# A two-layer squared-ReLU block on one core: the start of block 0, the loads of w1 and the shifted copies of x rearranged

## The chip, the core and the metric

The kernel runs on one core of a Trainium2 chip. The metric is the device time of one execution in microseconds (us), lower is better. The profile's span, from the first to the last instruction, is about 2 us shorter than that time (295.2 against 297.05 us for the profiled run).

Engines are named as in the profile: PE is TensorE's matmuls, PEld its weight loads, DVE is VectorE, ACT is ScalarE, POOL is GpSimd, SP is SyncE. SPq, ACTq and POOLq are their queues, which issue DMA transfers.

## What is computed

```python
# x [1, 2048, 576], w1 [576, 4608], b1 [4608], w2 [4608, 576], b2 [576], all bf16
h = jnp.einsum("bsd,df->bsf", x, w1) + b1
r = jnp.where(h > 0, h, 0)
h = r * r
out = jnp.einsum("bsf,fd->bsd", h, w2) + b2
```

The depth of the first product, 576, is four and a half times 128; that odd half shapes the whole kernel.

## The kernel before

The 2048 rows of x are cut into four blocks of 512 columns of the transposed x. The 4608 columns of w1 are cut into 36 f-tiles of 128. Phase A makes hT = relu(...)^2 for each block and f-tile; phase B multiplies hT with w2.

The depth of 576 is nine chunks of 64. TensorE is used as two halves of 64 rows: the lower 64 partitions work on one f-tile, the upper 64 on another, at the same time, each into a PSUM bank of its own. So w1 lies in SBUF as `w1h`: 64 partitions per half, nine chunks, and a step handles a pair of f-tiles. In the kernel before, pair j is f-tiles j and j + 18, as `w1h`'s lower half holds the first half of w1's columns and its upper half the second.

```python
P = 128; H = 64; NFT = 36; NJ = 18; NC = 4; NH = 9; DM = 512; SB = 512; NSB = 4; RT = 4; HALF = 256
def load_w1(eng, j0, j1):                   # two transfers of 64 partitions each
    for h in range(2):
        eng.dma_start(out=w1h[h * H:(h + 1) * H, :, j0 * P:j1 * P],
                      in_=w1_rows[:, :, h * FH + j0 * P:h * FH + j1 * P])
# ... cut ...
ORDER = ((0, 2, 4, 6, 8, 1, 3, 5, 7), (1, 3, 5, 7, 8, 2, 4, 6, 0))
def a_step(b, j):                           # one pair: 18 matmuls of 64 rows, two evictions
    bk = [bank("ph") for _ in range(2)]
    for i in range(NH):
        for h in range(2):
            c = ORDER[h][i]
            rows = slice(h * H, (h + 1) * H)
            nc.tensor.matmul(bk[h][:], lhsT=w1h[rows, c, j * P:(j + 1) * P],
                             rhs=xT[b][rows, place(h, c), :],
                             start=(i == 0), stop=(i == NH - 1))
    for h in range(2):
        evac_h(b, h * NJ + j, bk[h])        # ACT: relu + b1; DVE: square into hT
```

Each half needs all nine chunks of x on its own 64 partitions. Loaded naturally, even chunks lie on the lower half and odd ones on the upper, so some chunks have to be copied ("shifted") to the other half. For blocks 1 to 3 x comes by DMA transposes that fetch most of it twice, and two chunks are left to copy on VectorE at the start of each block:

```python
for b in range(1, NSB):
    nc.vector.tensor_copy(out=xT[b][0:H, 8, :], in_=xT[b][H:P, 7, :])   # line 228
    nc.vector.tensor_copy(out=xT[b][H:P, 8, :], in_=xT[b][0:H, 0, :])   # line 229
    for j in range(NJ):
        a_step(b, j)
    # ... cut: loads of w2 ...
```

Block 0 starts before transposed x and w1h are there. It loads x as it is (four tiles of 128 rows) and a "quad" of f-tiles as full 128-row chunks; it transposes x on TensorE, half a block (256 columns) at a time, and computes the quad with full-height matmuls. The last 64 rows of depth (the tail) are done with half-height ones. Chunk number 4 of `transpose_chunk` covers the last 128 columns of x and holds this tail in its upper half.

```python
quad = (0, 1, NJ, NJ + 1)                   # f-tiles 0, 1, 18, 19
load_x(nc.sync, 0);    load_x(nc.scalar, 1)
load_quad(nc.sync, 0); load_quad(nc.scalar, 1)   # each: 128 rows x two runs of 256 columns (512 B)
load_quad(nc.sync, 2); load_quad(nc.scalar, 3)
load_x(nc.sync, 2);    load_x(nc.sync, 3)
# ... cut: tail of the quad, identity, b1 and the tail of b2 by GpSimd, six warm-up matmuls ...
steps = [(half, c) for half in range(2) for c in range(NC + 1)]
transpose_chunk(0, 0, engs[0])              # two TensorE transposes, then a copy out of PSUM
for i, (half, c) in enumerate(steps):       # on VectorE and ScalarE in turn
    if i + 1 < len(steps):
        transpose_chunk(*steps[i + 1], engs[(i + 1) % 2])
    if c < NC:
        full_mm(half, c)                    # line 178: four matmuls of 256 columns
    elif half == 0:
        ...                                 # transposes b1 once
nc.vector.tensor_copy(out=xT[0][0:H, 8, :], in_=xT[0][H:P, 7, :])       # line 193, the tail
nc.vector.tensor_copy(out=xT[0][0:H, 4:7, :], in_=xT[0][H:P, 0:3, :])   # shifted copies
nc.vector.tensor_copy(out=xT[0][H:P, 4:7, :], in_=xT[0][0:H, 1:4, :])
nc.vector.tensor_copy(out=xT[0][H:P, 8, :], in_=xT[0][0:H, 0, :])
# ... cut: four tail matmuls (line 200) and the quad's evictions ...
for j0, j1 in ((2, 4), (4, 6), (6, 9), (9, 13), (13, 18), (0, 2)):
    load_w1(nc.sync, j0, j1)
# ... cut: DMA transposes of x for blocks 1 to 3, loads of b2 and w2, all on SyncE ...
for j in range(2, NJ):
    a_step(0, j)
```

Phase B is not changed, but for the column that holds b2's last 64 values and the place where block 3's hT lies (over w1h, by the pair's number).

Of the kernel before, what the change touches and what calls it, by code (L numbers as in the profile page):

```python
# [9 lines left out]
ACT = mybir.ActivationFunctionType  # L10
ALU = mybir.AluOpType
BF16 = mybir.dt.bfloat16
FP32 = mybir.dt.float32
# [4 lines left out]
def kernel(  # L18
# [9 lines left out]
    nc = tc.nc  # L28
    P = 128
    H = 64  # L30
    x2 = x.flatten_outer_dims()
    out2 = out.flatten_outer_dims()
    S, D = x2.shape
    F = w1.shape[1]
    FH = F // 2
    NFT = F // P
    NJ = NFT // 2
    NC = D // P
    NH = D // H
    DM = NC * P  # L40
    SB = 512
    NSB = S // SB
    RT = SB // P
    HALF = SB // 2
    XW = NH * SB
    assert D == DM + H and NH == 9 and NSB == 4 and NFT % 2 == 0

    ctx.enter_context(tc.manual_schedule())
    const = ctx.enter_context(tc.tile_pool(name="const", bufs=1))
# [6 lines left out]
    def bank(name):  # L56
        return psum.tile([P, SB], FP32, name=name, tag="bank")

    w1h = big.tile([P, NH, FH], BF16, name="w1h")
    hT = [big.tile([P, NFT, SB], BF16, name=f"hT{b}") for b in range(NSB - 1)]

    w2_sb = big.tile([P, NFT * D], BF16, name="w2_sb")
    at = [0]

    def early(n):
        at[0] += n
        assert at[0] <= NFT * D
        return w2_sb[:, at[0] - n:at[0]]  # L70


    xT = [early(XW).rearrange("p (w s) -> p w s", s=SB) for b in range(NSB - 1)]
# [2 lines left out]
    xs = early(RT * D).rearrange("p (j c) -> p j c", c=D)  # L76
    qn = early(NC * 4 * P).rearrange("p (c f) -> p c f", c=NC)
    qr = early(2 * P)
    quad = (0, 1, NJ, NJ + 1)

    x_view = x2.rearrange("(rt p) d -> p rt d", p=P)
    w1_halves = w1.rearrange("d (h f) -> d h f", h=2)
    w1_rows = w1.rearrange("(c p) f -> p c f", p=H)

    def w2(ft, a, b):
        return w2_sb[:, ft * D + a:ft * D + b]

    def load_x(eng, j):
        eng.dma_start(out=xs[:, j, :], in_=x_view[:, j, :])

    def load_quad(eng, c):
        eng.dma_start(out=qn[:, c, :].rearrange("p (h f) -> p h f", h=2),
                      in_=w1_halves[c * P:(c + 1) * P, :, 0:2 * P])

    def load_w1(eng, j0, j1):
        for h in range(2):
            eng.dma_start(out=w1h[h * H:(h + 1) * H, :, j0 * P:j1 * P],
                          in_=w1_rows[:, :, h * FH + j0 * P:h * FH + j1 * P])

    load_x(nc.sync, 0)  # L100
    load_x(nc.scalar, 1)
    load_quad(nc.sync, 0)
    load_quad(nc.scalar, 1)
    load_quad(nc.sync, 2)
    load_quad(nc.scalar, 3)
    load_x(nc.sync, 2)
    load_x(nc.sync, 3)
    for h in range(2):
        nc.sync.dma_start(out=qr[h * H:(h + 1) * H, :], in_=w1_halves[DM:D, h, 0:2 * P])

    ident = const.tile([P, P], BF16, name="ident")
    make_identity(nc, ident[:])
    b1_rows = const.tile([P, P], BF16, name="b1_rows")
    nc.gpsimd.memset(b1_rows[:], 0.0)
    nc.gpsimd.dma_start(out=b1_rows[0:NFT, :], in_=b1.rearrange("(ft p) -> ft p", p=P))
    for h in range(2):
        nc.gpsimd.dma_start(out=b1_rows[NFT:NFT + 1, h * H:(h + 1) * H],
                            in_=b2[DM:D].rearrange("(o d) -> o d", o=1))

    ones = nc.const_aps.tensor(1.0, [P, SB], BF16)  # L120
    wps = bank("wps")
# [4 lines left out]
    def copy_psum(eng, dst, src):  # L126
        if eng is nc.scalar:
            nc.scalar.copy(out=dst, in_=src)  # L128
        else:
            nc.vector.tensor_copy(out=dst, in_=src)  # L130

    def transpose_chunk(half, c, eng):
        d0 = c * P if c < NC else D - P
        cols = slice(half * HALF, (half + 1) * HALF)
        tp = psum.tile([P, HALF], BF16, name="tp", tag="bank")
        for i in range(2):
            nc.tensor.transpose(tp[:, i * P:(i + 1) * P], xs[:, 2 * half + i, d0:d0 + P], ident[:])  # L137
        copy_psum(eng, xT[0][:, c if c < NC else 7, cols], tp[:])

    def hT_of(b, ft):  # L140
        if b < NSB - 1:
            return hT[b][:, ft, :].rearrange("p (j s) -> p j s", j=RT)
        h, j = divmod(ft, NJ)
        return w1h[:, h * RT:(h + 1) * RT, j * P:(j + 1) * P]

    b1T = const.tile([P, NFT + 1], FP32, name="b1T")

    def evac_h(b, ft, bk):
        r = rpool.tile([P, SB], BF16, name="r", tag="r")
        nc.scalar.activation(out=r[:], in_=bk[:], func=ACT.Relu, bias=b1T[:, ft:ft + 1], scale=1.0)  # L150
        r3 = r[:].rearrange("p (j s) -> p j s", j=RT)
        nc.vector.tensor_tensor(out=hT_of(b, ft), in0=r3, in1=r3, op=ALU.mult)  # L152

    def place(hi, c):
        if hi:
            return c // 2 if c % 2 else (3 + c // 2 if c else 8)
        return 8 if c == 8 else (4 if c % 2 else 0) + c // 2

    ORDER = ((0, 2, 4, 6, 8, 1, 3, 5, 7), (1, 3, 5, 7, 8, 2, 4, 6, 0))

    def a_step(b, j):
        bk = [bank("ph") for _ in range(2)]
        for i in range(NH):
            for h in range(2):
                c = ORDER[h][i]
                rows = slice(h * H, (h + 1) * H)
                nc.tensor.matmul(bk[h][:], lhsT=w1h[rows, c, j * P:(j + 1) * P], rhs=xT[b][rows, place(h, c), :],  # L167
                                 start=(i == 0), stop=(i == NH - 1))
        for h in range(2):
            evac_h(b, h * NJ + j, bk[h])  # L170


    bk0 = [bank("ph") for _ in quad]

    def full_mm(half, c):
        cols = slice(half * HALF, (half + 1) * HALF)
# [2 lines left out]
                             start=(half == 0 and c == 0), stop=False, skip_group_check=True)  # L179

    engs = (nc.vector, nc.scalar)
    steps = [(half, c) for half in range(2) for c in range(NC + 1)]
    transpose_chunk(0, 0, engs[0])
    for i, (half, c) in enumerate(steps):
        if i + 1 < len(steps):
            transpose_chunk(*steps[i + 1], engs[(i + 1) % 2])
        if c < NC:
            full_mm(half, c)
        elif half == 0:
            b1T_ps = psum.tile([P, P], BF16, name="b1T_ps", tag="bank")  # L190
            nc.tensor.transpose(b1T_ps[:], b1_rows[:], ident[:])
            nc.vector.tensor_copy(out=b1T[:], in_=b1T_ps[:, 0:NFT + 1])
    nc.vector.tensor_copy(out=xT[0][0:H, 8, :], in_=xT[0][H:P, 7, :])
    nc.vector.tensor_copy(out=xT[0][0:H, 4:7, :], in_=xT[0][H:P, 0:3, :])
    nc.vector.tensor_copy(out=xT[0][H:P, 4:7, :], in_=xT[0][0:H, 1:4, :])
    nc.vector.tensor_copy(out=xT[0][H:P, 8, :], in_=xT[0][0:H, 0, :])
    for i in range(2):
        for h in range(2):
            rows = slice(h * H, (h + 1) * H)
            nc.tensor.matmul(bk0[2 * h + i][:], lhsT=qr[rows, i * P:(i + 1) * P], rhs=xT[0][rows, place(h, 8), :],  # L200
                             start=False, stop=True, skip_group_check=True)
        for h in range(2):
            evac_h(0, quad[2 * h + i], bk0[2 * h + i])


    for j0, j1 in ((2, 4), (4, 6), (6, 9), (9, 13), (13, 18), (0, 2)):
        load_w1(nc.sync, j0, j1)
    for b in range(1, NSB):
        rows = slice(b * SB, (b + 1) * SB)
        for i in range(2):  # L210
            nc.sync.dma_start_transpose(out=xT[b][:, i * NC:(i + 1) * NC, :], in_=x2[rows, i * H:i * H + DM])
    w2_view = w2_dram.rearrange("(ft p) d -> p ft d", p=P)
    W2CH = 6

    def load_w2(c):
        nc.sync.dma_start(out=w2_sb[:, c * W2CH * D:(c + 1) * W2CH * D].rearrange("p (ft d) -> p ft d", d=D),
                          in_=w2_view[:, c * W2CH:(c + 1) * W2CH, :])
# [2 lines left out]
    nc.sync.dma_start(out=b2_bc[:], in_=b2[0:DM].partition_broadcast(P))  # L220
    load_w2(4)
    load_w2(5)

    for j in range(2, NJ):
        a_step(0, j)
    load_w2(0)
    for b in range(1, NSB):
        nc.vector.tensor_copy(out=xT[b][0:H, 8, :], in_=xT[b][H:P, 7, :])  # L228
        nc.vector.tensor_copy(out=xT[b][H:P, 8, :], in_=xT[b][0:H, 0, :])
        for j in range(NJ):  # L230
            a_step(b, j)
        if b == 1:
            load_w2(1)
        if b == 2:
            load_w2(2)
            load_w2(3)


    oc = xpool.tile([P, NH, SB], BF16, name="oc", tag="xT3")
    o_tr = []  # L240
    for pr in range(NSB // 2):
        pc = bank("pc")
        for ft in range(NFT):
            for h in range(2):
                nc.tensor.matmul(pc[h * H:(h + 1) * H, :], lhsT=w2(ft, DM, D), rhs=hT_of(2 * pr + h, ft),  # L245
                                 start=(ft == 0), stop=(ft == NFT - 1))
        nc.scalar.activation(out=oc[:, pr, :], in_=pc[:], func=ACT.Identity, bias=b1T[:, NFT:NFT + 1], scale=1.0)  # L247
        o_tr.append(oc[:, 2 + pr, :].rearrange("p (j r) -> p j r", j=RT))
        nc.sync.dma_start_transpose(out=o_tr[pr], in_=oc[:, pr, :])

# [48 lines left out]
```

## Time and profile before

| what | value |
|---|---|
| time, median of 3 | 297.96 us (297.69 to 299.83) |
| span of the profiled run | 295.2 us |
| PE busy | 285.6 us, 97% |
| first full-height matmul of block 0 | 5.47 us after the span's start |
| first paired step | 11.46 us |
| end of phase A, first matmul of phase B | 152.08 us |
| DMA moved | 18.01 MB, mean 61 GB/s |

In the page and the views, a line of instructions gives start and duration in us, engine, source line, operation, output<-inputs, shape and count; what stands in brackets at the end is the idle time of that engine just before and what ended it. "Busy" for PE counts pipelined matmuls with modelled ends, so two matmuls in a row overlap; the cadence is read from starts, not from durations. A few matmul records are missing from a trace, so counts may be a little short.

### The profile page before, as it was taken

Reading aid. Unit: us, or ns where it says so; the run is one execution under the profiler, and the core shown is the slowest. Engines: PE = TensorE matmul, PEld = TensorE weight load, DVE = VectorE, ACT = ScalarE, POOL = GpSimd, SP = SyncE. Lnnn points to the kernel's source line nnn. Section 1 sums busy time; section 2 is a strip of 40 time slices with the busy share of each in tenths; the row PEclk is TensorE's granted clock in tenths of the full one; section 3 lists DMA queues with packets and bytes.
Section 4 is the critical chain, followed back from the end, with each engine's and each line's share of the span. In section 5 each row is a group of like instructions: output and inputs, shape, how many; then the busy total and the mean of one; then the engine's idle time right before and its main releaser. Section 6 shows DMA issues by size and latency. Waiting matters only on the chain.

```text
span 295.2 us, 4817 instructions
## 1 busy us (share of the span) xinstructions
PE 285.6 (97%) x2079; PEld 141.7 (48%) x2079; DVE 78.8 (27%) x193; ACT 95.5 (32%) x152; POOL 2.5 (1%) x10
## 2 busy tenths in 40 slices
PE   6999998999899998999999999999999999999996
PEld 3654444555455554555555444444444444444454
DVE  0644444444444445344440011000111111111111
ACT  2666665666656665566650000000000000000000
POOL 3000000000000000000000000000000000000000
PEclk9999999999999999999999999999999999999999
DMA  6999998910120003400000000000000000000000
GB/s 183 205 201 201 171 197 171 307 59 2 34 88 0 3 0 99 143 2 0 2 0 13 7 20 20 20 23 20 20 20 22 20 20 20 22 20 20 20 22 21
DMA packets 29909, 18.01 MB, mean 61 GB/s; under 512 B 14516, under 2 KB 29888, under 8 KB 29888
## 3 DMA queue, kind: packets, MB, share of 16 engines
q1 hardware_dynamic: 29104, 17.29, 26.3%
q10 hardware_dynamic: 688, 0.41, 0.5%
q8 instruction: 16, 0.26, 0.4%
q14 instruction: 5, 0.04, 0.0%
q0 software_dynamic: 96, 0.01, 0.0%
HBM read 11.94 MB, written 2.36 MB: 48 GB/s over the span
## 4 chain that ended last, share of the span: by engine, by line
PE 59%; DVE 0%; issue 0%
PE po L259 42%; PE ph L167 12%; PE pc L245 5%; DVE o_sb L261 0%
## 5 line engine op out<-in xcount | busy, mean ns | idle before, releaser
L150 ACT ACTIVATE r<-ph,b1T 128x512 bf16<-128x512 f32 x144 | 90.9, 684 | 51.8 <-PE ph L167 51.1
L167 PE MATMUL ph<-w_sb,w1h 64*128 64x512 bf16 x936 | 101.9, 376 | 2.4 <-DVE w_sb L228 2.3
L167 PEld LDWEIGHTS <-w1h 64*128 64x128 bf16 x1260 | 69.9, 94 | 70.7 <-issue 4.7
L259 PE MATMUL po<-w_sb,hT 128*128 128x512 bf16 x432 | 93.4, 379 | 0.0
L259 PEld LDWEIGHTS <-hT 128*128 128x128 bf16 x432 | 42.2, 98 | 51.2 <-issue 0.4
L152 DVE TENSOR_TENSOR hT<-r 128x512 bf16<-128x512 bf16 x108 | 45.9, 425 | 58.0 <-ACT r L150 57.7
L261 DVE TENSOR_TENSOR o_sb<-po,b_bc 128x512 bf16<-128x512 f32 (+2 forms) x17 | 11.2, 660 | 116.7 <-PE po L259 116.7
L167 PE MATMUL ph<-xT,w1h 64*128 64x512 bf16 x324 | 35.3, 376 | 1.3 <-DVE xT L228 1.3
L259 PE MATMUL po<-w_sb,w1h 128*128 128x512 bf16 (+2 forms) x180 | 31.3, 336 | 0.0
L259 PEld LDWEIGHTS <-w1h 128*128 128x128 bf16 x180 | 16.2, 98 | 15.3
L152 DVE TENSOR_TENSOR w1h<-r 128x512 bf16<-128x512 bf16 x36 | 15.3, 425 | 20.4 <-ACT r L150 20.4
L245 PE MATMUL pc<-hT,w_sb 128*64 128x512 bf16 x108 | 15.7, 379 | 0.0
L245 PEld LDWEIGHTS <-w_sb 128*64 128x64 bf16 x144 | 8.1, 110 | 7.6 <-issue 0.4
L245 PE MATMUL pc<-w1h,w_sb 128*64 128x512 bf16 x36 | 7.9, 379 | 0.0
L178 PE MATMUL ph<-w_sb 128*128 128x256 bf16 x32 | 4.6, 272 | 2.0 <-DMA w_sb<-in_w_dram 1.7
L247 ACT ACTIVATE oc<-pc,b1T 128x512 bf16<-128x512 f32 x2 | 1.4, 687 | 13.8 <-PE pc L245 13.8
L255 DVE COPY o_sb<-oc 128x64 bf16<-128x64 bf16 x16 | 2.7, 172 | 9.4 <-DMA oc<-oc 9.4
L178 PEld LDWEIGHTS <-w_sb 128*128 128x128 bf16 x32 | 2.9, 97 | 2.5 <-DMA w_sb<-in_w_dram 1.8
L130 DVE COPY w_sb<-tp 128x256 bf16<-128x256 bf16 x5 | 1.5, 291 | 8.0 <-PE tp L137 8.0
L128 ACT COPY w_sb<-tp 128x256 bf16<-128x256 bf16 x5 | 1.9, 373 | 5.0 <-PE tp L137 4.9
L124 PE MATMUL wps<-const-bfloat16-1.0 128*128 128x512 bf16 x6 | 2.7, 623 | 0.8 <-PEq L283 0.8
L137 PE MATMUL tp<-ident,w_sb 128*128 128x128 bf16 x20 | 2.6, 228 | 0.0
(25 smaller groups left out, 11.3 us busy)
## 6 DMA issues: line engine op xcount, KB each, us to landing
w_sb<-in_w_dram SPq DMA_DIRECT2D x6, 864.0 KB, 7.6
out_dram<-o_sb SPq DMA_DIRECT2D x15, 144.0 KB, 1.8
w1h<-in_w_dram SPq DMA_DIRECT2D x6, 288.0 KB, 6.3
w1h<-in_w_dram SPq DMA_DIRECT2D x2, 720.0 KB, 16.9
w1h<-in_w_dram SPq DMA_DIRECT2D x2, 576.0 KB, 13.4
w1h<-in_w_dram SPq DMA_DIRECT2D x2, 432.0 KB, 9.0
w_sb<-in_x_dram SPq DMA_DIRECT2D x3, 144.0 KB, 3.4
w_sb<-in_w_dram ACTq DMA_DIRECT2D x2, 128.0 KB, 3.7
```

The costliest lines, as they stand in the source:

```text
L124: nc.tensor.matmul(wps[:], lhsT=ones[:, 0:P], rhs=ones[:], start=(i == 0), stop=(i == NWARM - 1))
L128: nc.scalar.copy(out=dst, in_=src)
L130: nc.vector.tensor_copy(out=dst, in_=src)
L137: nc.tensor.transpose(tp[:, i * P:(i + 1) * P], xs[:, 2 * half + i, d0:d0 + P], ident[:])
L150: nc.scalar.activation(out=r[:], in_=bk[:], func=ACT.Relu, bias=b1T[:, ft:ft + 1], scale=1.0)
L152: nc.vector.tensor_tensor(out=hT_of(b, ft), in0=r3, in1=r3, op=ALU.mult)
L167: nc.tensor.matmul(bk[h][:], lhsT=w1h[rows, c, j * P:(j + 1) * P], rhs=xT[b][rows, place(h, c), :], start=(i == 0), stop=(i == NH - 1))
L178: nc.tensor.matmul(bk0[q][:, cols], lhsT=qn[:, c, q * P:(q + 1) * P], rhs=xT[0][:, c, cols], start=(half == 0 and c == 0), stop=False, ski ...
L245: nc.tensor.matmul(pc[h * H:(h + 1) * H, :], lhsT=w2(ft, DM, D), rhs=hT_of(2 * pr + h, ft), start=(ft == 0), stop=(ft == NFT - 1))
L255: nc.vector.tensor_copy(out=o_sb[:, DM:D], in_=o_tr[pr][:, jj, h * H:(h + 1) * H])
L259: nc.tensor.matmul(po[:, 0:e - a], lhsT=hT_of(b, ft)[:, jj, :], rhs=w2(ft, a, e), start=(ft == 0), stop=(ft == NFT - 1))
L261: nc.vector.tensor_tensor(out=o_sb[:, a:e], in0=po[:, 0:e - a], in1=b2_bc[:, a:e], op=ALU.add)
```

## The change

Five things are moved at once; the arithmetic is the same, apart from the order in which partial sums are added.

1. Block 0's quad is f-tiles 0 to 3, neighbours in memory, so a row of a quad load is one run of 1 KB. The pairs follow: (0, 2), (1, 3), and then f with f + 4 in groups of four.
2. w1 comes in groups of four pairs with runs of 1 KB (two pairs last). The lower halves are issued on SyncE, the upper halves on GpSimd, the first group in two parts (five and four chunks). These loads are issued early in the program, before the warm-up matmuls; x's fourth tile moves from SyncE's queue to ScalarE's.
3. In block 0's start, the tail chunk is transposed second instead of last, and its shifted copy is taken straight out of PSUM. The remaining shifted copies of block 0 are no longer ahead of the tail matmuls.
4. Pairs 2 to 5 of block 0 run their first five steps one pair after the other, and then their last four, in eight banks, so that the chunks that need a shifted copy come later.
5. The two copies that complete x for block b + 1 move from the start of that block to the middle of block b (for block 1: after pair 14 of block 0). b2's last 64 values get a column of their own.

```diff
-    quad = (0, 1, NJ, NJ + 1)
+    pairs = [(0, 2), (1, 3)] + [(f, f + G) for f in range(G, NFT) if (f // G) % 2]     # G = 4
     def load_quad(eng, c):
-        eng.dma_start(out=qn[:, c, :].rearrange("p (h f) -> p h f", h=2),
-                      in_=w1_halves[c * P:(c + 1) * P, :, 0:2 * P])
+        eng.dma_start(out=qn[:, c, :], in_=w1[c * P:(c + 1) * P, 0:G * P])
-    load_x(nc.sync, 3)
+    load_x(nc.scalar, 3)
+    def load_w1(eng, h, j0, n, cs):
+        f0 = pairs[j0][h] * P
+        eng.dma_start(out=w1h[h * H:(h + 1) * H, cs, j0 * P:(j0 + n) * P], in_=w1_rows[:, cs, f0:f0 + n * P])
+    w1_first = ((slice(0, 9, 2), slice(1, 8, 2)), (slice(1, 8, 2), slice(0, 9, 2)))
+    for part in range(2):
+        for h, eng in enumerate((nc.sync, nc.gpsimd)):
+            load_w1(eng, h, 2, G, w1_first[h][part])
+    for m in range(1, 4):
+        for h, eng in enumerate((nc.sync, nc.gpsimd)):
+            load_w1(eng, h, 2 + G * m, G, slice(0, NH))
 ... cut ...
         copy_psum(eng, xT[0][:, c if c < NC else 7, cols], tp[:])
+        if c == NC:
+            nc.vector.tensor_copy(out=xT[0][0:H, 8, cols], in_=tp[H:P, :])
 ... cut ...
-    steps = [(half, c) for half in range(2) for c in range(NC + 1)]
-    transpose_chunk(0, 0, engs[0])
-    for i, (half, c) in enumerate(steps):
-        if i + 1 < len(steps):
-            transpose_chunk(*steps[i + 1], engs[(i + 1) % 2])
-        if c < NC:
-            full_mm(half, c)
+    n = 0
+    for half in range(2):
+        ahead = [0, NC, 1, 2, 3]
+        lead = 3 if half == 0 else 2
+        for i in range(lead):
+            transpose_chunk(half, ahead[i], engs[n % 2])
+            n += 1
+        for c in range(NC):
+            full_mm(half, c)
+            if lead + c < NC + 1:
+                transpose_chunk(half, ahead[lead + c], engs[n % 2])
+                n += 1
 ... cut: b1's transpose after half 0; the four tail matmuls ...
-    nc.vector.tensor_copy(out=xT[0][0:H, 8, :], in_=xT[0][H:P, 7, :])      # was ahead of the tail matmuls
+    # the other shifted copies of block 0 stand after the tail matmuls
-    for j0, j1 in ((2, 4), (4, 6), (6, 9), (9, 13), (13, 18), (0, 2)):
-        load_w1(nc.sync, j0, j1)
+    for h, eng in enumerate((nc.sync, nc.gpsimd)):
+        load_w1(eng, h, 0, 2, slice(0, NH))
 ... cut ...
-    for j in range(2, NJ):
-        a_step(0, j)
+    bks = {}
+    for j in range(2, 2 + G):
+        bks[j] = [bank("ph") for _ in range(2)]
+        a_part(0, j, bks[j], range(5))          # a_part: the given steps of a_step's loop
+    for j in range(2, 2 + G):
+        a_part(0, j, bks[j], range(5, NH))
+        for h in range(2):
+            evac_h(0, pairs[j][h], bks[j][h])
+    for j in range(2 + G, NJ):
+        a_step(0, j)
+        if j == NJ - 4:
+            finish_xT(1)                        # finish_xT(b): the two copies of lines 228 and 229
     for b in range(1, NSB):
-        nc.vector.tensor_copy(out=xT[b][0:H, 8, :], in_=xT[b][H:P, 7, :])
-        nc.vector.tensor_copy(out=xT[b][H:P, 8, :], in_=xT[b][0:H, 0, :])
         for j in range(NJ):
             a_step(b, j)
+            if j == NJ // 2 and b + 1 < NSB:
+                finish_xT(b + 1)
```

The aims: longer runs and two issuing queues for w1, work for TensorE while the shifted copies of block 0 are made, and no copies at the seams between blocks.

## The prediction

> **What bounds the kernel now.** I read the page's busy shares first, then the list of waits, then TensorE's own timeline, then a table of stages for the DMA rate.
>
> ```profile
> span 295.2 us, 4817 instructions
> PE 285.6 (97%) x2079; PEld 141.7 (48%) x2079; DVE 78.8 (27%) x193; ACT 95.5 (32%) x152; POOL 2.5 (1%) x10
> ```
>
> TensorE is busy 285.6 of 295.2 us. The change removes no matmul, so it can only take from the 9.6 us in which TensorE stands idle, or spend more of them. The list of waits says where they are:
>
> ```profile
> PE ph L167 <- DVE w_sb L228: 2.3, 2, 1.2
> ...
> PE ph L178 <- DMA w_sb<-in_w_dram: 1.7, 1, 1.7
> PE ph L167 <- DVE xT L228: 1.3, 1, 1.3
> ...
> PEld L167 <- DMA w1h<-in_w_dram: 0.5, 1, 0.5
> ```
>
> (Columns: us in total, times, longest us.) Three stalls at the starts of blocks 1, 2 and 3, behind the shifted x copy of line 228, sum to 3.6 us. One stall of 1.7 us is for the first w1 quad. The only wait for w1h itself is 0.5 us, and that is on the weight-load side, so w1's supply does not bound block 0. TensorE's timeline puts the stalls in order (start, length, what, idle before):
>
> ```profile
> 3.29 0.52 PE L137 MATMUL tp<-ident,w_sb 128*128 128x128 bf16 x4
> 5.47 0.61 PE L178 MATMUL ph<-w_sb 128*128 128x256 bf16 x4 [1.66 <-DMA w_sb<-in_w_dram]
> ...
> 7.80 0.28 PE L137 MATMUL tp<-ident,w_sb 128*128 128x128 bf16 x2
> 8.37 0.60 PE L178 MATMUL ph<-w_sb 128*128 128x256 bf16 x4 [0.29 <-ACT w_sb L128]
> ...
> 11.03 0.61 PE L200 MATMUL ph<-w_sb 64*128 64x512 bf16 x4 [0.35 <-DVE w_sb L193]
> 11.46 32.54 PE L167 MATMUL ph<-w_sb,w1h 64*128 64x512 bf16 x296
> 45.09 35.14 PE L167 MATMUL ph<-w_sb,w1h 64*128 64x512 bf16 x324 [1.09 <-DVE w_sb L228]
> 81.48 34.28 PE L167 MATMUL ph<-w_sb,w1h 64*128 64x512 bf16 x316 [1.25 <-DVE w_sb L228]
> ```
>
> The reader is to see two things: a start phase up to 11.46, where the paired steps begin, and then an unbroken stream with a hole at each block. The cadence comes from block 3: its last 316 matmuls run from 117.87 to 152.08 us, 0.1083 us each, so a pair (18 of them) takes 1.95 us. From the hole of block 2 to that of block 3 is 117.87 - 81.48 = 36.39 us, and 324 matmuls need 35.08: a hole costs 1.31 us.
>
> The DMA rate while w1 alone is moving:
>
> ```profile
> 16.00:28.00 12.00, 11.95 (x111) 5.88 (x109) 5.11 (x12) 7.71 (x13) 0.00 (x0) 1.00 1.12 201
> ```
>
> The last column is 201 GB/s. In this stretch the runs are 1 KB and longer (pairs 9 to 18), yet in the stretches from 4 to 6 us, where x and the quads fill 128 partitions, the same view gives 314 and 291 GB/s. It is the 64 partitions, not the run length, that go with 200.
>
> [...] So the kernel before gives a rate: 0.68 us for the b1 load of 36 runs, 0.50 us for each b2 load of 16 runs, hence (0.68 - 0.50) / 20 = 9 ns per run on 0.35 us. It is a thin estimate, from two sizes far below those to come.
>
> **Part 1, the shifted copies move into mid-block.** The copies for block b+1 (two of 0.29 us) now sit behind pair 9 of block b, and those for block 1 behind pair 14 of block 0. Per pair ScalarE needs 2 x 0.64 and VectorE 2 x 0.43 us of the 1.95 us, so 0.58 us more fits beside them with the four r buffers. Block 1's transposed x must have landed by then (about 37 us), or VectorE stops in order behind it. Before, SyncE began these transposes at 23.8 us, after 12 w1 loads; now it has six, half the bytes, so they come earlier. All three holes close: 1.31 + 1.31 + 1.15 (block 1's idle is 1.09) = **3.8 us gained**.
>
> **Part 2, block 0's start.** I compute T, the start of the first paired step (11.46 before), from F, the start of the first full-height matmul (5.47 before).
> - F waits for quad 0. Its runs are 1 KB instead of 512 B[...], but at 4 to 6 us the DMA moved about 300 GB/s already. I choose 0.35 us earlier: F = 5.1.
> - Half 0: two chunks and the tail are transposed ahead, in the idle time before F. Then 16 matmuls at 0.108 = 1.73, two transposed chunks at 0.12, b1's at 0.06, and some 0.1 of waiting: 2.1 us (2.33 before).
> - Half 1: here the order of TensorE's instructions decides. Only chunk 0 and the tail are ahead, and each next chunk is transposed directly in front of the matmuls that use it. The kernel before had one chunk's matmuls in between. From the start of a transpose to the matmul that uses it the trace has 6.46 to 7.20 = 0.74 us through a ScalarE copy, and 5.91 to 6.57 = 0.66 through VectorE (some of it behind the matmuls between; 0.60 by its parts, 0.31 + 0.29). So: chunk 0 0.74 + 0.43 of matmuls, chunk 1 0.74 + 0.43, chunk 2 (VectorE) 0.60 + 0.43, chunk 3 0.74 + 0.43, and the four tail matmuls 0.43: 4.97 us. Before, 7.80 to 11.46 = 3.66. **1.3 us lost.** It would have been worse by the 0.35 us wait for L193, which is gone, as the tail is now copied straight out of PSUM.
> - x2 and x3 must be there at F + 2.1 = 7.2. GpSimd's w1 loads now run at the same time, at 1 KB per 9 ns, about 110 GB/s, from some 4 us on. By 4 us 0.53 MB have moved (53 + 276 + 202 GB/s), so 0.58 MB of x and quads are left at perhaps 200 GB/s: 6.9, and with 0.6 to land 7.5 us. I add 0.3.
> T = 5.1 + 2.1 + 0.3 + 5.0 = **12.5, a loss of 1.0 us**.
>
> **Part 3, the grouped steps.** The first five steps of each of pairs 2 to 5 need no shifted copy except x's tail, so TensorE has 40 matmuls (4.3 us) of work before the 0.55 us copies matter. All eight banks are taken: pair 4 waits for the first two evictions, ready about T + 1.4 and needed at T + 2.2; pair 5 needs two more at T + 3.25, ready at T + 2.7. No stall. GpSimd's second load (chunks 0 to 8 even, upper half) is needed at T + 0.9 = 13.4. Generation: 2.4 + 0.35 + 256 x 0.009, then 0.35 + 320 x 0.009, ends at 8.3; the b1 load landed 3.5 us after its issue began, so 12 us. Later groups cost 0.35 + 576 x 0.009 = 5.5 us each and are eaten every 7.8. No stall, with 1.4 us to spare at the first. The rate asked is 1.18 MB / 7.8 us = 151 GB/s, under 201. So faster w1 supply is worth **0**, as nothing waited for it.
>
> **Part 4, b2's tail** goes to a column of its own: two small loads and a 128x1 copy, beside other work: 0.
>
> Sum: -3.8 + 1.0 = -2.8 from 297.96: **295.2 us**.
>
> **Rivals.** *GpSimd's generation becomes the bound.* If a run costs 20 ns and not 9, 576 of them take 11.9 us against 7.8, and block 0 stretches by over 10 us. For it: [...] the thinness of the 9 ns. Against it: the measured small loads. It would give 300 to 315 us; I give it one in sixteen. *The start gains.* If the quads land at 4.5 and x2, x3 keep up, T is 11.6 and the whole 3.8 us are kept: 294.2; with a shorter half 1 (the copies' latency partly hidden) 293.4. To pass 2% (292.0) it would need T below 9.3, which the 5 us of half 1 forbid. *Contention hits x2 and x3.* If w1 takes half of the DMA from 4 us on, they land at 8.5, T is 13.5 to 14, and 296.5 remain. *The mid-block copies are too early for block 1's x.* Then VectorE, ScalarE and, beyond the buffers, TensorE wait; it would cost part of 1.15 us.
>
> **Range and chances.** The hole term is nearly certain (within 0.4); T is uncertain from 11.4 to 13.5, which gives 293.6 to 296.7, and a little for the GpSimd tail: 293.4 to 297.2. Faster by over 2% is 0.04, within 2% 0.90, slower by over 2% 0.06.
>
> **What would show it.** Right: no wait of PE for the shifted copies at blocks 1 to 3; four waits of PE for copies of chunks in half 1, about 0.3 us each; the first paired matmul at about 12.5. Wrong: PEld waiting for w1h in block 0, GpSimd's DMA instructions of 576 runs lasting over 8 us, or half 1 in under 4 us.

## The result, and the profile after

| | median of four, us | lowest to highest |
|---|---|---|
| before | 298.69 | 297.69 to 299.83 |
| changed | 302.87 | 302.45 to 303.53 |

Changed over before is 1.0141, 95% interval 1.0091 to 1.019: slower, by less than 2%, and outside the predicted range. The page of the changed kernel: first its span and busy shares, then the second view (40 slices of 7.5 us each, with TensorE's granted clock in tenths), then the queues of the third view (packets, MB, share of 16 engines; q1 is SyncE's, q0 GpSimd's) and the chain that ended last.

```profile
span 300.7 us, 4814 instructions
PE 290.1 (96%) x2068; PEld 133.9 (45%) x2079; DVE 79.4 (26%) x195; ACT 95.0 (32%) x152; POOL 6.9 (2%) x16
...
PEclk9659999999999999999999999999999999999999
...
q1 hardware_dynamic: 24576, 14.49, 20.4%
q0 software_dynamic: 848, 2.66, 4.0%
...
PE ph L175 46%; PE po L299 41%; PE pc L285 5%; DMA w1h<-in_w_dram 5%; DMA w_sb<-in_x_dram 1%; SPq L110 0%; DVE o_sb L301 0%
```

For comparison, GpSimd's queue and the chain of the kernel before:

```profile
q0 software_dynamic: 96, 0.01, 0.0%
...
PE po L259 42%; PE ph L167 12%; PE pc L245 5%; DVE o_sb L261 0%
```

Three things are new. GpSimd's queue moves 2.66 MB. The second and third slice have lost some of the clock, which was 9 tenths or more throughout before. And the chain, which before was TensorE back to 118 us and no further, now runs back through a w1h load (5% of the span) to an x load issued at 0.74 us, for which SyncE waited before its next issue. The waits of TensorE name a w1h load and an x load; the three waits at the seams of blocks are gone:

```profile
PE ph L175 <- DMA w1h<-in_w_dram: 3.0, 1, 3.0
PE tp L144 <- DMA w_sb<-in_x_dram: 1.8, 1, 1.8
...
PE ph L190 <- ACT w_sb L135: 1.2, 3, 0.5
```

TensorE's own timeline (start, length, idle before in brackets) places them:

```profile
4.46 1.01 PE L190 MATMUL ph<-w_sb 128*128 128x256 bf16 x4
...
7.28 0.22 PE L208 MATMUL b1T_ps<-ident,b_rows 128*128 128x128 bf16 x1
9.32 0.76 PE L144 MATMUL tp<-ident,w_sb 128*128 128x128 bf16 x4 [1.82 <-DMA w_sb<-in_x_dram]
...
15.31 1.01 PE L190 MATMUL ph<-w_sb 128*128 128x256 bf16 x4 [0.46 <-ACT w_sb L135]
16.25 1.04 PE L213 MATMUL ph<-w_sb 64*128 64x512 bf16 x4
20.27 39.91 PE L175 MATMUL ph<-w_sb,w1h 64*128 64x512 bf16 x356 [2.98 <-DMA w1h<-in_w_dram]
```

Half 0 is done at 7.3 us, and then x's third and fourth tile (x2 and x3) are missing until 9.3. Half 1 takes from 9.3 to 17.3. Its groups of four matmuls last 1.01 us in place of 0.60: the clock is halved (0.50 granted from 10 to 20 us). Then a w1 load is missing until 20.3. Phase B starts at 157.66 us. The profiled runs split as follows:

| stretch | before, us | changed, us | difference |
|---|---|---|---|
| start to first paired step | 11.46 | 20.27 | +8.8 |
| first paired step to phase B | 140.62 | 137.39 | -3.2 |
| phase B to the end | 143.12 | 143.04 | -0.1 |

So the middle gained, and the start lost more. Which load was late? The DMA answers, by the time of issue (KB each, median us from issue to landing):

```profile
w1h<-in_w_dram POOLq DMA_DIRECT2D x1, 320.0 KB, 7.9
w1h<-in_w_dram SPq DMA_DIRECT2D x1, 320.0 KB, 15.2
```

The two 320 KB transfers of the first group are alike but for the queue, the half of the partitions and the time of issue. GpSimd's was issued at 3.1 us. SyncE's, issued at 5.0 us, landed at 20.2; that is when the paired steps begin. x2 and x3, issued at 2.1 us, took 7.1 and 7.4 us.

### The profile page after: what moved, and what is told of

It reads as the page before. It is cut to its first block, busy times and chain, and to the rows that moved or that the text cites. A ratio compares the mean times of both kernels' runs of the same rounds, so it can differ in the third digit from the quotient of the medians.

```text
span 300.7 us, 4814 instructions
## 1 busy us (share of the span) xinstructions
PE 290.1 (96%) x2068; PEld 133.9 (45%) x2079; DVE 79.4 (26%) x195; ACT 95.0 (32%) x152; POOL 6.9 (2%) x16
## 3 DMA queue, kind: packets, MB, share of 16 engines
q0 software_dynamic: 848, 2.66, 4.0%
## 4 chain that ended last, share of the span: by engine, by line
PE 92%; DMA 6%; SPq 0%; issue 0%; DVE 0%
PE ph L175 46%; PE po L299 41%; PE pc L285 5%; DMA w1h<-in_w_dram 5%; DMA w_sb<-in_x_dram 1%; SPq L110 0%; DVE o_sb L301 0%
## 5 line engine op out<-in xcount | busy, mean ns | idle before, releaser
L175 PEld LDWEIGHTS <-w1h 64*128 64x128 bf16 x1260 | 60.5, 95 | 80.3 <-DMA w1h<-in_w_dram 3.9
L190 PE MATMUL ph<-w_sb 128*128 128x256 bf16 x32 | 6.9, 365 | 1.5 <-ACT w_sb L135 1.2
L287 ACT ACTIVATE oc<-pc,b2T 128x512 bf16<-128x512 f32 x2 | 1.4, 687 | 13.7 <-PE pc L285 13.7
L144 PE MATMUL tp<-ident,w_sb 128*128 128x128 bf16 x20 | 3.6, 298 | 1.9 <-DMA w_sb<-in_x_dram 1.8
L190 PEld LDWEIGHTS <-w_sb 128*128 128x128 bf16 x32 | 3.9, 126 | 3.3 <-issue 2.2
L99 POOL DMA_DIRECT2D w1h<-in_w_dram x6 | 4.3, 748 | 0.0
## 6 DMA issues: line engine op xcount, KB each, us to landing
w1h<-in_w_dram SPq DMA_DIRECT2D x1, 320.0 KB, 15.2
```

The costliest lines, as they stand in the source:

```text
L99: eng.dma_start(out=w1h[h * H:(h + 1) * H, cs, j0 * P:(j0 + n) * P], in_=w1_rows[:, cs, f0:f0 + n * P])
L190: nc.tensor.matmul(bk0[q][:, cols], lhsT=qn[:, c, q * P:(q + 1) * P], rhs=xT[0][:, c, cols], start=(half == 0 and c == 0), stop=False, ski ...
```

## The experiments

Theory A: GpSimd's w1 stream takes most of the DMA engines' time, so x2, x3 and SyncE's first w1 part starve. The rivals are that grouped 64-partition loads are slow whatever the queue (B), that the lower partitions are the slow side (C), and that the halved clock is the main loss (D). Ratios are to the kernel before, with 95% intervals; medians of before were 298.75 to 299.04 us in these comparisons.

**All of w1 on SyncE.**

```diff
-    for h, eng in enumerate((nc.sync, nc.gpsimd)):   # three places
+    for h, eng in enumerate((nc.sync, nc.sync)):
```

> The changed kernel with the upper halves of w1 back on SyncE's queue (same groups, same 1 KB runs, same place in the program). Theory A: GpSimd's stream takes most of the DMA and so delays x2, x3 and SyncE's first w1 part; with one queue in order, x2 and x3 land before 7.5 us, the first paired step starts at 12 to 13 us (20.3 in the changed kernel), and the time is 295 to 296.5 us, under the kernel before. Theory B: w1 in groups of four with transfers of 64 partitions is itself too slow, whichever queue has it; then the first part still lands after 15 us and the time stays above 300 us.

Measured: 293.44 us, ratio 0.9807 (0.9787 to 0.9827). TensorE's timeline of this kernel:

```profile
4.29 1.01 PE L190 MATMUL ph<-w_sb 128*128 128x256 bf16 x4
...
7.41 0.39 PE L144 MATMUL tp<-ident,w_sb 128*128 128x128 bf16 x4
8.14 0.60 PE L190 MATMUL ph<-w_sb 128*128 128x256 bf16 x4 [0.35 <-ACT w_sb L135]
...
9.31 0.60 PE L190 MATMUL ph<-w_sb 128*128 128x256 bf16 x4 [0.46 <-ACT w_sb L135]
...
12.10 0.60 PE L213 MATMUL ph<-w_sb 64*128 64x512 bf16 x4
12.54 47.65 PE L175 MATMUL ph<-w_sb,w1h 64*128 64x512 bf16 x440
```

x2 and x3 land within 4.4 and 4.5 us, half 1 starts at 7.41 without a wait for DMA, and the first paired step stands at 12.54. The same 320 KB transfers now take 5.0 us each:

```profile
w1h<-in_w_dram SPq DMA_DIRECT2D x2, 320.0 KB, 5.0
```

The time is 1.6 us under the range that I had expected. B falls. One word in each of three loops, the name of the queue, is worth 9.4 us between the medians (302.87 to 293.44).

**The halves swapped.**

```diff
-    for h, eng in enumerate((nc.sync, nc.gpsimd)):   # three places
+    for h, eng in enumerate((nc.gpsimd, nc.sync)):
```

> The changed kernel with the queues swapped: lower halves on GpSimd, upper halves on SyncE. Theory A (the queue decides): now the upper halves land late, SyncE's first w1 part again after 15 us, and the first paired step starts at 19 to 22 us; the time is 301 to 305 us. Theory C (the lower 64 partitions are the slow side, or it is the larger first part): the lower halves land late even from GpSimd, and SyncE's land early.

Measured: 305.0 us, ratio 1.0194 (1.0147 to 1.0241). Now the upper halves are late: SyncE's parts land 14.3 and 17.6 us after their issue, at about 19.3 and 23.3, and TensorE waits for both. GpSimd's, to the lower half, take 7.6 and 8.0 us.

```profile
17.66 0.63 PE L175 MATMUL ph<-w_sb,w1h 64*128 64x512 bf16 x1
19.34 1.89 PE L175 MATMUL ph<-w_sb,w1h 64*128 64x512 bf16 x8 [1.04 <-DMA w1h<-in_w_dram]
23.37 36.86 PE L175 MATMUL ph<-w_sb,w1h 64*128 64x512 bf16 x324 [2.14 <-DMA w1h<-in_w_dram]
```

The lateness goes with SyncE's queue, not with the partitions: C falls.

**Fillers that keep the clock up**, in two sizes.

```diff
+    def filler(count):                    # matmuls on constants into a bank of their own
+        fb = bank("fill")
+        for i in range(count):
+            nc.tensor.matmul(fb[:], lhsT=ones[:, 0:P], rhs=ones[:], start=(i == 0), stop=(i == count - 1))
+        if half == 1: filler(8)           # second size: 6
+    filler(24)                            # after the tail matmuls; second size: 14
```

> The changed kernel with 8 filler matmuls of 512 columns in front of half 1's transposes and 24 after the four tail matmuls, so that TensorE does not stand idle while it waits and its granted clock stays at 1.0. Theory A: the end of the wait is SyncE's first w1 part, which lands at about 20 us either way; so only the cold matmuls after 20.3 us get faster and the time falls by 1 to 2 us, to 301 to 302. Theory D (the halved clock from 9.4 to 22.5 us is the main loss): the time falls by 4 us or more, to under 299 us.

Measured: 301.62 us, ratio 1.01 (1.0065 to 1.0134). But in its trace the 24 fillers ran until 23.0 us, beyond the landing of SyncE's part at about 19.8, so they set the start themselves. Hence the second size:

> The fillers of the run before ended after SyncE's first w1 part had landed, and so set the end of the wait themselves; here they are shorter, 6 and 14 matmuls. Theory A (SyncE's first w1 part ends the wait): the first paired step starts at 19.5 to 21 us, as in the changed kernel, half 1 takes 5 us in place of 7, and the time is 300.5 to 302 us. Theory D (the halved clock is the main loss): the first paired step starts before 17 us and the time is under 299 us.

Measured: 303.27 us, ratio 1.0126 (1.0075 to 1.0177), 1.3 us over the upper end of what I expected. Its timeline:

```profile
10.08 0.64 PE L144 MATMUL tp<-ident,w_sb 128*128 128x128 bf16 x4 [0.22 <-DMA w_sb<-in_x_dram]
...
15.02 0.61 PE L221 MATMUL ph<-w_sb 64*128 64x512 bf16 x4
15.56 3.23 PE L199 MATMUL fill<-const-bfloat16-1.0 128*128 128x512 bf16 x13
20.91 39.41 PE L175 MATMUL ph<-w_sb,w1h 64*128 64x512 bf16 x348 [2.12 <-DMA w1h<-in_w_dram]
```

Half 1 at full clock takes 5.4 us (7.8 in the changed kernel) and its tail is done at 15.6, yet the paired steps wait until 20.9 for the same load. So the halved clock of half 1 lay beside that wait and cost nothing. D falls.

**Only the seams**: the kernel before, with nothing but the copies for the next block moved.

```diff
     for j in range(2, NJ):
         a_step(0, j)
+        if j == NJ - 2:
+            finish_xT(1)
     for b in range(1, NSB):
-        # the two copies for block b stood here
         for j in range(NJ):
             a_step(b, j)
+            if j == NJ // 2 and b + 1 < NSB:
+                finish_xT(b + 1)
```

> The kernel before with only the two shifted copies per block moved into the middle of the block before (behind pair 9; for block 1 behind pair 16 of block 0, as its transposed x lands at about 41 us). All else as before. By the prediction's hole term of 3.8 us the time is 294.5 to 295.5 us, and TensorE waits for VectorE at no seam. Rival: the holes are filled by another wait (banks or r buffers) and less than 2 us is gained.

Measured: 294.35 us, ratio 0.9828 (0.9791 to 0.9864). No wait for VectorE at a seam is left.

```profile
13.60 46.58 PE L167 MATMUL ph<-w_sb,w1h 64*128 64x512 bf16 x430
...
149.69 8.17 PE L251 MATMUL pc<-hT,w_sb 128*64 128x512 bf16 x73
```

From the first paired step (13.60) to phase B (149.69) are 136.09 us, against 140.62 before: the seams cost 4.5 us. Its start was slower than that of the profiled kernel before, 13.60 against 11.46, on the same instructions: the matmuls of half 0 ran at half pace until about 9.8 us (1.04 us for four, 0.61 before), though the granted-clock column reads 1.00 there.

**GpSimd's loads held back** until x2 and x3 are there.

```diff
+    held = const.tile([P, 2, 1], BF16, name="held")
+    nc.gpsimd.tensor_copy(out=held[:], in_=xs[:, 2:4, 0:1])    # in GpSimd's order ahead of its w1 loads
```

> The changed kernel with GpSimd's w1 loads held back until x2 and x3 have landed (a tiny GpSimd copy that reads both stands in front of them). Theory A: x2 and x3 land before 7.5 us again and half 1 starts by 7.6; SyncE's first part, issued some 2 us ahead of GpSimd's stream, lands before 11 us; the first paired step starts between 12.3 and 14.5 us, but SyncE's later groups then starve behind GpSimd's 2.4 MB, and a stall of 2 to 5 us comes within block 0, before 26 us. Time 296 to 300 us. Rival E (only the early start of GpSimd's stream was harmful, the queues share evenly): no stall in block 0, 293 to 294.5 us.

Measured: 297.98 us, ratio 0.995 (0.9923 to 0.9977); the profiled run took 295.76. x2 and x3 land by 6.3 us again, and the tail is done at 12.0. The stall comes, 2.3 us in sum and before 26 us, but behind another load than I had expected:

```profile
12.02 0.38 PE L177 MATMUL ph<-w_sb,w1h 64*128 64x512 bf16 x1
13.56 1.04 PE L177 MATMUL ph<-w_sb,w1h 64*128 64x512 bf16 x8 [1.16 <-DMA w1h<-in_w_dram]
15.76 44.42 PE L177 MATMUL ph<-w_sb,w1h 64*128 64x512 bf16 x410 [1.16 <-DMA w1h<-in_w_dram]
```

It waits for GpSimd's own first two parts, issued at 6.7 and 7.4 us and landed at 13.5 and 15.8. SyncE's second group, issued at 6.4, landed at 16.5 and was in time. So rival E does not hold, but I had the wrong load starving: what had been issued ahead on SyncE still got through, and GpSimd's first parts took 6.8 and 8.4 us. The runs spread from 295.59 to 299.21 us, and their mean granted clock falls with them: 1.000 in the three shortest, 0.994 in the middle, 0.989 in the four longest. What lowered it in the longer ones has no trace and stays open.

**The first group's upper half on ScalarE's queue**, all else of w1 on SyncE.

```diff
     for part in range(2):
-        for h, eng in enumerate((nc.sync, nc.gpsimd)):
+        for h, eng in enumerate((nc.sync, nc.scalar)):
```

> All w1 on SyncE, but the two upper parts of the first group on ScalarE's queue. Theory A (what harms is GpSimd's share of the DMA, not a second queue): the two queues share evenly, SyncE's and ScalarE's first parts both land before 11 us, the first paired step starts at 12 to 13 us, 293 to 295 us. Rival F (any second queue beside SyncE's starves it): SyncE's first part lands more than 3 us later than ScalarE's, and the first paired step starts after 14 us.

Measured: 298.39 us, ratio 0.9995 (0.9973 to 1.0018). SyncE's first part landed at about 10.6 us, ScalarE's, issued 1.4 us earlier, at about 8; the two second parts both landed at about 13. So by its landings F falls. But the time and the first paired step missed, for a reason that has nothing to do with shares: these loads held ScalarE itself. The two issues took 0.69 and 0.63 us, with 1.3 us between them.

```profile
3.75 2.62 ACTq L99 DMA_DIRECT2D w1h<-in_w_dram  x2
6.41 1.28 ACT L135 ACT_TABLE_LOAD   x1 [6.41 <-DMA w_sb<-in_w_dram]
7.70 0.65 ACT L135 COPY w_sb<-tp 128x256 bf16<-128x256 bf16 x2
```

Its first copy out of PSUM came at 7.70 us (4.32 in the changed kernel), and the first paired step at 17.32.

**The shares by themselves.** A kernel that only loads:

```diff
+    # three stages, each after the one before has landed; per queue two transfers to 64 partitions
+    # 1: GpSimd 64x9x512 twice, SyncE 64x9x512 twice          runs of 1 KB
+    # 2: GpSimd as in 1,        SyncE 64x2x2048 and 64x3x2048  SyncE's runs 4 KB
+    # 3: ScalarE 64x9x512 twice, SyncE 64x9x512 twice         runs of 1 KB
```

> The disputed share by itself; nothing is computed, and the output is zeros. Three stages one after the other, each with two queues that start together and load about 1.2 MB of w1 each in two transfers to 64 partitions: (1) SyncE lower and GpSimd upper half, all runs 1 KB; (2) the same with SyncE's runs 4 KB (1.3 MB); (3) SyncE and ScalarE, all runs 1 KB. In the changed kernel GpSimd's queue moved 2.65 MB in some 750 packets (3.5 KB each), SyncE's packets are single runs. Theory A (the DMA engines take one packet of each queue in turn): in stage 1 both GpSimd transfers land before SyncE's first; in stage 2 the two queues land about together; in stage 3 too. Rival G (GpSimd's queue is preferred whatever the packets): stage 2 looks like stage 1. Rival H (the lower half is slow): SyncE is last in all three.

By landing order stage 1 was not as expected: SyncE's first transfer landed at 6.3 us, GpSimd's first at 9.1, the second ones at 12.9 (GpSimd) and 13.1. GpSimd's packets only began to flow at 4.7 us, 3.5 us after its first issue, so SyncE had the engines to itself at first. Stages 2 and 3 have the same order, with SyncE's first transfer 5.2 to 5.7 us after the stage's first issue and the other queue's 8.1 to 8.4, so landings do not tell the theories apart. The shares do, where both queues flow steadily. Counted from the DMA packet records of the traces (packets of 512 B and more, by their ends):

```
kernel, stretch in us            GpSimd GB/s, packets/us    other queue GB/s, packets/us
changed, 14 to 18                207, 50.5                  SyncE 57, 55.5
GpSimd held back, 14 to 24       201, 49.5                  SyncE 55, 53.6
loads only, stage 1, 9.5-11.5    205, 50.0                  SyncE 55, 54.0    (1 KB runs)
loads only, stage 2, 20.5-23.5   120, 29.3                  SyncE 165, 40.3   (4 KB runs)
loads only, stage 3, 33 to 36    ScalarE 153, 149.3         SyncE 162, 158.7  (1 KB runs)
```

With 1 KB runs on SyncE both queues complete about the same number of packets per us in these stretches, but GpSimd's packets are 4096 B (its 1 KB runs are joined by fours) and SyncE's are single runs of 1 KB: four fifths of the bytes are GpSimd's. With 4 KB runs SyncE holds its own (165 against 120 GB/s). Theory A's turns, one packet of each queue, fit the stretches with 1 KB runs: 50.5 against 55.5 packets per us in the changed kernel, 149.3 against 158.7 in stage 3. G falls by these shares, and H because SyncE's first transfer, to the lower half, lands first in all three stages.

Equal turns are not the whole account. In stage 2 SyncE has 40.3 packets per us against 29.3. Counted in the same way, the changed kernel from 6 to 9 us has 38.7 packets per us on GpSimd's queue, 16.3 on SyncE's and 11.7 on ScalarE's. In stage 3 ScalarE's first transfer flows nearly alone from 30.5 to 32.5 us (215.5 packets per us against 12.0), though SyncE's second one had been issued at 26.7. Of the 15.2 us of SyncE's first w1 part in the changed kernel, 7.1 pass before its first packet moves, at 12.1 us; till then its queue is still moving x2 and the quad's tail. Equal turns fit only what comes after. A rival for the time before is that transfers issued earlier, as GpSimd's were, go first. The held-back run fits it (SyncE's parts, issued first there, landed in 4.4 and 4.9 us), but no run sets it apart, and it stays open.

**Toward a better version.** All of w1 on SyncE, and three chunks ahead in half 1 too.

```diff
-        lead = 3 if half == 0 else 2
+        lead = 3
```

> All w1 on SyncE as in the first run, and in half 1 three chunks transposed ahead, as in half 0, so that each chunk's copy out of PSUM lies beside the matmuls of the chunk before. By the prediction's working half 1 shrinks by about 1.2 us (5.1 to 3.9), the first paired step starts at 11.2 to 11.6 us, if w1 is there, and the time is 292 to 292.6 us. Rival: w1's second upper part (landing at about 12.3) then ends the wait, and less than 0.5 us is gained.

Measured: 293.49 us, ratio 0.9827 (0.9781 to 0.9872): no gain over all of w1 on SyncE. The profiled run is the longest of four (295.32 us; the others lie from 293.26 to 293.67). In it half 1 did shrink, and the first paired matmul stands at 10.33 us, but nine matmuls later TensorE waits for w1's second upper part until 13.51:

```profile
10.33 1.49 PE L175 MATMUL ph<-w_sb,w1h 64*128 64x512 bf16 x9
13.51 46.75 PE L175 MATMUL ph<-w_sb,w1h 64*128 64x512 bf16 x416 [1.69 <-DMA w1h<-in_w_dram]
```

The rival was right: w1's supply had become the bound. So the step that needs this part should come later:

```diff
-        a_part(0, j, bks[j], range(5))          # first pass over pairs 2 to 5
+        a_part(0, j, bks[j], range(4))
-        a_part(0, j, bks[j], range(5, NH))
+        a_part(0, j, bks[j], range(4, NH))
```

> All w1 on SyncE, three chunks ahead in half 1 (as in the run before, whose start then waited 1.7 us for w1's second upper part), and the first pass over pairs 2 to 5 cut to four steps, so that the step which needs that part comes 3.5 us after the first paired step and not 0.9. Expected: no wait for w1h, the first paired step at 10.3 to 11 us, the rest as in the run with all w1 on SyncE (136.1 us to phase B): 291 to 292 us. Rival: w1's first parts land only at about 11.5, and then the time is as before this step, 293.3.

Measured: 292.33 us, ratio 0.9826 (0.9764 to 0.9889; one run of four, at 295.51, widens it, the other three lie from 292.24 to 292.38).

```profile
10.03 0.60 PE L213 MATMUL ph<-w_sb 64*128 64x512 bf16 x4
10.47 8.15 PE L175 MATMUL ph<-w_sb,w1h 64*128 64x512 bf16 x73
18.98 11.18 PE L175 MATMUL ph<-w_sb,w1h 64*128 64x512 bf16 x102 [0.36 <-DMA w1h<-in_w_dram]
```

The start is at 10.47 us as expected; the time is just over the range. One new wait comes at the next group of w1: the supply is now just short there. Its median is the lowest of all kernels tried, 1.1 us under the one with all of w1 on SyncE; but the ratios to the kernel before, 0.9826 and 0.9807, do not tell the two apart.

## Why the prediction was wrong

The prediction was 295.2 us; the time is 302.87, 7.7 us more. It forecast 2.8 us less than the kernel before, and 4.2 us more were measured. Its 0.90 for a change of less than 2% came true by luck, since the terms that it named do not give that sum. Its steps one by one:

- **Part 1, the seams: right in kind, small in size.** All three holes closed. The term was 3.8 us and measured 4.5: from 140.62 to 136.09 us in the run with the seams alone. I had set the cadence at 0.1083 us from block 3; without holes 1260 matmuls in 136.09 us make 0.1080. (With both halves of TensorE at work, a matmul of 64 rows and 512 columns starts as often as a full-height one of 256 columns: four of those take 0.43 us in block 0 of the kernel before, from 8.37 to 8.80.) Then the holes of blocks 2 and 3 are 1.40 each, and block 0 with its seam (33.63 us for 296 matmuls, 31.97 by that cadence) another 1.66.
- **Part 2, F and half 0: two errors that nearly cancel.** F came at 4.46 us and not at 5.1, as quad 0, issued at 1.2 us in both kernels, landed 3.0 us later and not 4.2. Half 0 took 2.8 us and not 2.1, because its first matmuls ran at half pace (1.01 us for four of 256 columns, 0.60 later; the granted-clock column reads 1.00 there, and the reason is open).
- **Part 2, half 1: right.** In the run with all of w1 on SyncE it takes 7.41 to 12.54 = 5.13 us, predicted 4.97, with the four waits for copies that were named. The run with three chunks ahead confirms the cause: 6.86 to 10.33 = 3.5 us.
- **Part 2, x2 and x3: the first place where the failed step shows.** It said that GpSimd's loads run "at 1 KB per 9 ns, about 110 GB/s", and so x2 and x3 would be there at 7.5 us (0.6 of it to land; in the kernel before x3's last packet ended at 6.23 us by the packet records, and x3 landed at 6.79). The pace per run was read from the durations of GpSimd's instructions for two small loads, of 36 and 16 runs (the prediction calls this time generation), and it does not exist:

```profile
L99 POOL DMA_DIRECT2D w1h<-in_w_dram x6: 682/770/775, 2.4 to 5.9; - x6
```

(Minimum, median and maximum duration in ns, first and last start in us.) Loads of 256 to 576 runs all took 0.68 to 0.78 us, like the one of 36 runs. By 6.7 us GpSimd had issued all of its 2.65 MB, and nothing seen paced them but the DMA engines, which were busy throughout (share 0.99 to 1.13 from 6 to 9 us). Of these it took 158 GB/s from 6 to 9 us, leaving 13 each to SyncE's and ScalarE's queues. x2 and x3 landed at about 9.4. This delay alone cost nothing in the end: with fillers half 1 was done at 15.6 us, and the paired steps still started at 20.9.
- **Part 3: here the failed step set the time.** I worked out that GpSimd's upper parts would come in time ("no stall, with 1.4 us to spare") and set faster supply at 0, and never asked what GpSimd's loads would do to SyncE's lower parts. The first of these landed at 20.2 us, when the first paired step was to be at 12.5, and the page's chain goes through that very load. These 7.7 us are nearly all of the error: 0.7 us more gained at the seams and 1.3 us lost to matmuls at half clock are the other terms. (In the profiled spans the error is 8.3 us, by the medians 7.0, as the profiled run of the kernel before, at 297.05 us, lay under its median of 298.69.) One sign of being wrong that the prediction named came with it, PEld's wait for w1h in block 0, of 3.9 us.
- **The rivals.** "GpSimd's generation becomes the bound" looked for harm in the wrong direction: not too slow, but too fast. That its 300 to 315 us hold the measured time is luck. "Contention hits x2 and x3" was the right kind, but took an even split and stopped at x; it gave 296.5.
- **What was right is borne out by undoing the rest.** With all of w1 on SyncE the first paired step is at 12.54 us, where 12.5 was predicted; that it is so close is in part luck, as F (4.29) and half 0 (3.1 us) miss in opposite directions there too. From that kernel (293.44) to the changed one (302.87) are 9.4 us, the cost of the queue: 7.7 of later start and 1.3 of matmuls at half clock after it (137.39 against 136.07 us to phase B) are seen in the profiled runs, 9.0 of span in all.

## What to carry to other kernels

A transfer's queue is a claim on the shared DMA engines (here GpSimd's moved 158 GB/s from 6 to 9 us, and 13 were left to each of the other two): before moving loads to another queue, ask for each load already there what it will now wait behind, and set the bytes per packet of the two queues side by side (here 4096 against 1024, and 207 against 57 GB/s from 14 to 18 us). A cost per item that is read from two small cases is no cost model; if the whole plan hangs on it, ask also what happens when it is zero. And when an early stage waits, see which wait ends last: here a full clock through half 1 gained nothing, and one queue's name changed 9 us.

## What the runs showed of the hardware that I had not expected

Two streams to the two halves of the partitions do run side by side, and together they move more than one. The stages of the changed kernel (the last column is GB/s), first with both halves flowing and then with the lower half alone:

```profile
14.00:18.00 4.00, 2.83 (x13) 1.09 (x11) 1.17 (x3) 1.48 (x3) 0.00 (x0) 0.50 1.06 260
21.00:25.00 4.00, 4.00 (x30) 1.61 (x28) 0.00 (x0) 0.00 (x0) 0.00 (x0) 0.75 1.14 193
```

And in the kernel that only loads, stage 3, with even shares:

```profile
33.00:36.00 3.00, 0.15 (x1) 0.00 (x0) 1.00 1.10 315
```

That is 193 GB/s for one half, 260 for an uneven mix and 315 for an even one, 63% more. In the kernel that only loads, one half nearly alone moved 233 GB/s (30.5 to 32.5 us), and against that the even mix is 35% more.

A gap of 1.8 us in TensorE's work (7.5 to 9.3 us) was followed by half clock from about 9.4 until past 20 us (0.50 granted from 10 to 20), though TensorE was busy for 5.74 of those 10 us. With the second size of fillers the granted clock was 1.00 through half 1. The gap of 1.7 us in the run with three chunks ahead was followed by the same (0.73 from 12 to 16 us); two gaps of 1.2 us in the profiled held-back run were not (1.00). The same start also ran at half or full pace from run to run (half 0 of the kernel before and of the seams run, 0.61 and 1.04 us for its first four matmuls, at 1.00 in the granted-clock column); half 0 took 4.2 us in the seams run and 2.3 before.
